# Sequence transform first on untransposed input, and DMA transposes for most of the MLP's input, in a gated FFT/MLP kernel

## The chip, the cores and the metric

The kernel runs on one core of a Trainium2 chip. The metric is the device time of one execution in microseconds (us). The profile's span is the time from the first to the last instruction of the core.

Engine names are those of the profile: PE is the matrix engine, PEld its weight loads, ACT, DVE and POOL are the scalar, vector and GpSimd engines, SP is the engine that does nothing but issue DMA in these kernels (its timeline shows nothing else). A "q" behind a name (SPq) stands for DMA issues on that engine's queue. R, PX and `w_sb` are shared buffers, so one name can stand for several tensors.

## The reference

```python
# x [2048, 512], w_r and w_i [2048, 257], w1 [512, 1792], w2 [1792, 512], all bf16
g = sigmoid((x * gate_w).sum(-1, keepdims=True))
X = rfft2(x.astype(float32)) * (w_r + 1j * w_i)
a = irfft2(X, s=(2048, 512)).astype(bfloat16)
h = x @ w1 + b1
b = (h * tanh(softplus(h))) @ w2          # Mish between two matmuls
return g * a + (1 - g) * b
```

## The kernel before

The two-dimensional FFT is done by matmuls with constant matrices. The d-transform goes over the 512 features. The sequence of 2048 is split as 128 × 16: the p-transform goes over 128 positions, and a "middle stage" does the 16 that remain and multiplies with W. The data between p-transform and middle stage has to change its layout, and goes through a DRAM scratch buffer for that. After the middle stage it goes through a second scratch buffer, and the inverse transforms follow. PE is filled with MLP matmuls wherever the transform chain waits.

A list scheduler in Python plans the order of instructions on each engine when the kernel is built. It knows only modelled durations, and sees the DMA as one first-in first-out pipe with a fixed rate. The planned order is then built into the program.

```python
DMA_BW = 390e3                       # planner's idea of the DMA rate, bytes per us
...
x_sb = R1[:].rearrange("p (t d) -> p t d", t=NT)          # 16 tiles of x, 128 rows each
...
# w1 and x: loads on SP's queue
t_w1 = ld_w1(1)                      # the last of them
# constants (W_r, W_i, SM; then w2, GD), GpSimd's queue, start when t_w1 has landed
wload("wr", Wa, A_w_r, "Wa")
wload("wi", Wb, A_w_i, "Wb")
dma("ld_sm", SM[:], ..., deps=[t_w1], queue="pool")
for h in range(2):
    dma(f"ld_w2_{h}", ..., deps=[t_w1], queue="pool")
dma("ld_gd", GD[:], ..., deps=[t_w1], queue="pool")
```

Each tile is first transposed on PE. Its sums and differences (butterflies) and its d-transform work on the transposed tile, then the p-transform follows:

```python
for t in range(NT):
    ...
    for dt_ in range(4):             # PE transposes (L598), then an eviction to xT on DVE or ACT
        ins = e.transpose(psb[:, bk(sl), 128*dt_:128*(dt_+1)], x_sb[:, t, 128*dt_:128*(dt_+1)], ident[:, :])
    ...
    bfly("bd", XB[:, 2:4, tr_, :], xT[:, 0:2, tr_, :], xT[:, 2:4, tr_, :], ALU.subtract, ...)
    bfly("bs", xss, xT[:, 0:2, tr_, :], xT[:, 2:4, tr_, :], ALU.add, ...)
    ...
# d-transform (L633 to L636): writes runs of 64 neighbouring PSUM columns
e.matmul(o[:, :, 2:4, :], XB[:, 2, t, :], f4(256), start=True, stop=False)
e.matmul(o[:, :, 2:4, :], XB[:, 3, t, :], f4(512), start=False, stop=True)
e.matmul(o[:, :, 0, :], XB[:, 0, t, :], f2(0), start=True, stop=True)
return e.matmul(o[:, :, 1, :], XB[:, 1, t, :], f2(128), start=True, stop=True)
# eviction, then the p-transform (L645)
return e.matmul(ps[:, bk(sl), :], FT[:, t, :], In1[:, t, :], start=True, stop=True)
# eviction; every fourth tile a scratch write
dma(f"r1w{t // 4}", scr1_w[...], A1s[...], 128 * 4096, ...)
```

The gate needs the transposed form of the whole of x, and so does the MLP:

```python
for t in range(NT):                  # gate, L664: 64 small matmuls as one task
    for dt_ in range(4):
        ins = e.matmul(ps[:, bk(sl_g), t:t+1], xT[:, dt_, t, :], gw_sb[:, dt_:dt_+1], ...)
...
for h in range(4):                   # scratch reads
    dma(f"r1r{h}", In2[...], scr1_r[...], 128 * 4096, reads=[("scr1", i) for i in range(4)], ...)
# first middle-stage matmul, L733
e.matmul(ps[:, bk(sx), 0:256], MI["RFe"], In2[:, 0, :], start=True, stop=True)
...
# first MLP layer, L785: one "group" is four of these; Mish is L793; second layer is L803
ins = e.matmul(ps[:, bk(sl), :], w1_sb[:, dt_, 128*ft:128*(ft+1)], xT[:, dt_, 4*c:4*c+4, :], ...)
```

## Time and profile before

| | before |
|---|---|
| time, median of 3 runs | 153.02 us (152.56 to 154.95) |
| span of the profiled run | 151.8 us |
| PE busy | 92% of the span |
| share of the chain of waits on PE | 86% |
| first middle-stage matmul | 51.0 us |

From the page of the kernel before: the span, three rows of its slice table (40 slices of 3.8 us, a digit is tenths), the chain by engine, two groups (line, engine, operation, count, then busy us and mean ns, then idle time before them), and one kind of DMA issue (count, size, median us to landing).

```profile
span 151.8 us, 2262 instructions
...
PE   0479998979999999999999999999999999999990
...
PEclk9999998799999999999999999999999999999999
DMA  4999399999993920303030399013010000101011
...
PE 86%; ACT 6%; DMA 4%; DVE 2%; issue 0%; SPq 0%; DVEq 0%
...
L785 PE MATMUL ps<-xT,w_sb 128*128 128x512 bf16 x224 | 52.8, 383 | 1.1 <-ACT hsb L793 1.0
...
L598 PE MATMUL ps<-ident,R 128*128 128x128 bf16 x64 | 5.8, 247 | 6.1 <-DMA R<-in_A_x_dram 6.0
...
scr<-R SPq DMA_DIRECT2D x8, 512.0 KB, 6.7
```

PE is near full from the tenth slice to the end. A PE that is full and on the chain for 86% of the span is the bound. What a change of the front part can win lies in the first nine slices alone. The 6.1 us ahead of the transposes (L598) are waits for x. The DMA is near full in eleven of the first fourteen slices, up to about 53 us.

Two further views show what the front part ends with. First the chain of waits of the kernel before, in order of time (start us, length us, what, count):

```profile
40.65 10.38 PE ps L785 x48
51.03 0.26 PE ps L733
...
124.18 24.19 PE ps L803 x112
```

Then one line of its waits (who, for what, total us, times, longest us):

```profile
PEld ps L733 <- DMA R<-scr: 0.5, 1, 0.5
```

PE does MLP groups until 51.03 us and then starts the middle stage, whose weight load (PEld) waits 0.5 us for the scratch read.

### The profile page before, as it was taken

To read this page: it belongs to the slowest core of one execution; us is meant where nothing else is said; L and a number is where in the kernel's file an instruction comes from. 1 tells how busy PE (TensorE), PEld (TensorE's weight loads), DVE (VectorE), ACT (ScalarE), POOL (GpSimd) and SP (SyncE) were. 2 spreads that over 40 slices of the span, in tenths; PEclk is the share of its full clock that TensorE was granted. 3 is DMA by queue.
4 is the path that set the end of the run, shared out by engine and by line. 5 is a ranking of instruction groups with operands and counts; after the bars stand their busy time and mean duration, and the time that the engine had idled before them with its cause. 6 is when DMAs were issued, how large, how long until landed. Compare 5 with 4: busy or idle time off the path is not lost.

```text
span 151.8 us, 2262 instructions
## 1 busy us (share of the span) xinstructions
PE 139.3 (92%) x850; PEld 73.0 (48%) x850; DVE 79.6 (52%) x173; ACT 75.5 (50%) x125; POOL 11.1 (7%) x21
## 2 busy tenths in 40 slices
PE   0479998979999999999999999999999999999990
PEld 0345666633444444444444445666676444444440
DVE  0183699769400487995954003899679301123111
ACT  2043884699787573433475863254798770000000
POOL 1050694001000000000000000000000000000000
PEclk9999998799999999999999999999999999999999
DMA  4999399999993920303030399013010000101011
GB/s 124 320 420 358 71 248 212 148 220 395 397 293 76 384 104 0 138 0 138 0 138 4 147 278 266 0 69 118 24 71 4 0 0 0 69 0 69 22 52 71
DMA packets 14207, 20.68 MB, mean 136 GB/s; under 512 B 788, under 2 KB 10420, under 8 KB 14132
## 3 DMA queue, kind: packets, MB, share of 16 engines
q1 hardware_dynamic: 12544, 14.81, 29.2%
q0 software_dynamic: 1328, 5.38, 13.5%
q10 hardware_dynamic: 324, 0.33, 1.0%
q8 instruction: 7, 0.11, 0.3%
q14 instruction: 4, 0.03, 0.1%
HBM read 14.23 MB, written 6.29 MB: 135 GB/s over the span
## 4 chain that ended last, share of the span: by engine, by line
PE 86%; ACT 6%; DMA 4%; DVE 2%; issue 0%; SPq 0%; DVEq 0%
PE ps L803 32%; PE ps L785 31%; PE ps L851 5%; DMA R<-in_A_x_dram 4%; ACT R L509 3%; PE ps L832 2%; PE ps L598 2%; PE ps L759 2%; PE ps L735 2%; PE ps L760 2%; PE ps L633 2%; PE ps L634 1%; ACT hsb L793 1%; PE ps L664 1%; PE ps L645 1%; ACT L793 1%
## 5 line engine op out<-in xcount | busy, mean ns | idle before, releaser
L785 PE MATMUL ps<-xT,w_sb 128*128 128x512 bf16 x224 | 52.8, 383 | 1.1 <-ACT hsb L793 1.0
L803 PE MATMUL ps<-w_sb,hsb 128*128 128x512 bf16 x224 | 51.0, 379 | 0.0
L793 ACT ACTIVATE hsb<-ps,b1f 128x512 bf16<-128x512 f32 x56 | 37.9, 689 | 11.5 <-PE ps L785 11.1
L803 PEld LDWEIGHTS ps<-w_sb,hsb 128*128 128x128 bf16 x224 | 21.7, 98 | 24.9
L785 PEld LDWEIGHTS ps<-xT,w_sb 128*128 128x128 bf16 x224 | 21.3, 99 | 25.4 <-ACT hsb L793 2.3
L509 ACT ACTIVATE R<-ps 128x512 bf16<-128x512 f32 (+1 forms) x27 | 15.6, 595 | 13.6 <-PE ps L760 7.1
L508 DVE CAST R<-ps 128x512 bf16<-128x512 f32 (+1 forms) x21 | 14.0, 689 | 11.6 <-PE ps L760 6.4
L882 DVE SCALAR_TENSOR_TENSOR R<-ps,omg,R 128x512 bf16<-128x512 f32 x8 | 6.0, 750 | 23.6 <-PE ps L803 23.6
L746 DVE TENSOR_TENSOR PX<-ps,Wa 128x256 bf16<-128x256 f32 x32 | 11.9, 414 | 10.8 <-PE ps L734 10.5
L746 DVE TENSOR_TENSOR PX<-ps,Wb 128x256 bf16<-128x256 f32 x32 | 11.9, 412 | 0.0
L598 PE MATMUL ps<-ident,R 128*128 128x128 bf16 x64 | 5.8, 247 | 6.1 <-DMA R<-in_A_x_dram 6.0
L813 ACT ACTIVATE R<-ps,omg 128x512 bf16<-128x512 f32 x8 | 5.5, 687 | 10.3 <-PE ps L803 10.3
L842 ACT ACTIVATE TT<-ps 128x512 bf16<-128x512 f32 x13 | 7.5, 593 | 4.9 <-PE ps L832 3.2
L851 PE MATMUL ps<-GD,TT 128*128 128x256 bf16 x64 | 8.9, 273 | 0.0
L598 PEld LDWEIGHTS ps<-ident,R 128*128 128x128 bf16 x64 | 4.7, 112 | 7.3 <-DMA R<-in_A_x_dram 6.3
L874 DVE SCALAR_TENSOR_TENSOR R<-ps,gcol,PX 128x256 bf16<-128x256 f32 x16 | 7.7, 482 | 0.6
L607 ACT ACTIVATE xT<-ps 128x512 bf16<-128x512 bf16 x11 | 5.8, 612 | 4.2 <-PE ps L598 4.1
L875 DVE SCALAR_TENSOR_TENSOR R<-ps,ngcol,PX 128x256 bf16<-128x256 f32 x16 | 7.6, 475 | 0.0
L851 PEld LDWEIGHTS ps<-GD,TT 128*128 128x128 bf16 x64 | 6.1, 98 | 2.8 <-ACT TT L842 0.2
L839 DVE CAST TT<-ps 128x512 bf16<-128x512 f32 x3 | 2.0, 685 | 9.5 <-PE ps L832 9.5
L859 DVE SCALAR_TENSOR_TENSOR PX<-ps,gcol,R 128x512 f32<-128x512 f32 x8 | 6.0, 744 | 1.3 <-PE ps L851 1.3
L633 PE MATMUL ps<-FD,R 128*128 128x256 bf16 x16 | 5.4, 341 | 1.1 <-DVE R L618 1.1
(95 smaller groups left out, 105.4 us busy)
## 6 DMA issues: line engine op xcount, KB each, us to landing
scr<-R SPq DMA_DIRECT2D x8, 512.0 KB, 6.7
R<-scr SPq DMA_DIRECT2D x8, 512.0 KB, 5.5
out_dram<-R SPq DMA_DIRECT2D x8, 256.0 KB, 2.0
w_sb<-in_B_w_dram SPq DMA_DIRECT2D x2, 896.0 KB, 9.4
w_sb<-in_B_w_dram POOLq DMA_DIRECT2D x2, 896.0 KB, 17.9
R<-in_A_x_dram SPq DMA_DIRECT2D x3, 512.0 KB, 9.1
SM<-c_sm POOLq DMA_DIRECT2D x1, 640.0 KB, 14.4
Wa<-in_A_w_r_dram POOLq DMA_DIRECT2D x1, 514.0 KB, 5.5
```

The lines of the kernel that those rows point to most:

```text
L508: G.add(name, [("dve", dve_dur(n), lambda e: e.tensor_copy(out=outf(), in_=inf())), ("act", act_dur(n), lambda e: e.activation(outf(), inf ...
L509: ("act", act_dur(n), lambda e: e.activation(outf(), inf(), AF.Copy))],
L598: ins = e.transpose(psb[:, bk(sl), 128 * dt_:128 * (dt_ + 1)], x_sb[:, t, 128 * dt_:128 * (dt_ + 1)], ident[:, :])
L633: e.matmul(o[:, :, 2:4, :], XB[:, 2, t, :], f4(256), start=True, stop=False)
L746: ins = e.tensor_tensor(out=po, in0=px, in1=pw, op=ALU.mult)
L785: ins = e.matmul(ps[:, bk(sl), :], w1_sb[:, dt_, 128 * ft:128 * (ft + 1)], xT[:, dt_, 4 * c:4 * c + 4, :], start=(dt_ == 0), stop=(dt_ == 3))
L793: return e.activation(hsb[:, hb, ft, :], ps[:, bk(sl), :], AF.Mish, bias=b1f[:, ft:ft + 1])
L803: ins = e.matmul(ps[:, bk(sl), :], hsb[:, hb, ft, 128 * tl:128 * (tl + 1)], w2_sb[:, ft, :], start=(ft == 0), stop=(ft == NFT - 1))
L842: return e.activation(TT[:, st.i, :, :].rearrange("p a b -> p (a b)"), ps[:, bk(sk), :], AF.Copy)
L851: ins = e.matmul(ps[:, bk(sy), 256 * hh:256 * (hh + 1)], TT[:, st.i, i, :], GD[:, i, :], start=(i % 2 == 0), stop=(i % 2 == 1))
L874: e.scalar_tensor_tensor(out=ya[:, t, 0:256], in0=ps[:, bk(sy), 256:512], scalar=gcol[:, t:t + 1], in1=tE[:, se.i, 0:256], op0=ALU.mult, o ...
L875: return e.scalar_tensor_tensor(out=ya[:, t, 256:512], in0=ps[:, bk(sy), 256:512], scalar=ngcol[:, t:t + 1], in1=hi, op0=ALU.mult, op1=ALU ...
```

## The change

Its intent is to start the transform chain earlier. If the p-transform goes first, it contracts over the rows of x and needs no transposed input. The four 128-column matmuls per tile use the butterflied tile as the stationary operand, so their output comes out transposed, as the d-transform wants it. Then only the gate and the MLP need xT, and 12 of its 16 tiles are fetched by transposing DMA instead of PE transposes with evictions. The d-transform can write its outputs in natural column order with strides of 2 and 4, and the multiplies with W become simple 512-column operations. Two smaller things change with it: the first loads are reordered, and Mish no longer waits for the gate's tanh.

The diff, cut to its core:

```diff
+XBAR_BW = 230e3
...
         t_w1 = ld_w1(1)
+        for t in range(4, NT):
+            dma(f"ld_xt{t}", xT[:, :, t, :], xv[:, t, :], 128 * 1024, writes=[("xT", t)], bw=XBAR_BW, transpose=True)
...
-        for t in range(NT):
+        def tr(t):                     # PE transpose of one tile and its eviction, as before
...
+            if t < 4:
+                tr(t)
...
-                bfly("bs", xss, xT[:, 0:2, tr_, :], xT[:, 2:4, tr_, :], ALU.add, 256 * n, xr, [("xs", hv)])
+                xa, xb = x_sb[:, tr_, 0:256], x_sb[:, tr_, 256:512]
+                t_x1.append(bfly("bs", xss, xa, xb, ALU.add, 256 * n, xr, [("xs", hv)]))
...
+            def f_s1(e, t=t, sl=sl):   # p-transform first, output transposed
+                for i in range(4):
+                    ins = e.matmul(ps[:, bk(sl), 128 * i:128 * (i + 1)], XB[:, t, i, :], FT[:, t, :], start=True, stop=True)
...
             def f_a1(e, t=t, sl=sl):
-                e.matmul(o[:, :, 2:4, :], XB[:, 2, t, :], f4(256), start=True, stop=False)
-                e.matmul(o[:, :, 2:4, :], XB[:, 3, t, :], f4(512), start=False, stop=True)
-                e.matmul(o[:, :, 0, :], XB[:, 0, t, :], f2(0), start=True, stop=True)
-                return e.matmul(o[:, :, 1, :], XB[:, 1, t, :], f2(128), start=True, stop=True)
+                e.matmul(o[:, :, 1::2], In1[:, t, 256:384], fd(256, 256), start=True, stop=False)
+                e.matmul(o[:, :, 1::2], In1[:, t, 384:512], fd(512, 256), start=False, stop=True)
+                e.matmul(o[:, :, 0::4], In1[:, t, 0:128], fd(0, 128), start=True, stop=True)
+                return e.matmul(o[:, :, 2::4], In1[:, t, 128:256], fd(128, 128), start=True, stop=True)
...
-                G.add(f"{nm}_{gp}", [("dve", 2 * dve_dur(256), f_w)], ...)
+                G.add(f"{nm}_{gp}", [("dve", dve_dur(512), f_w)], ...)
...
-                G.add(f"hs_{c}_{ft}", ..., reads=[sl, "b1f", "gth"], ...)
+                G.add(f"hs_{c}_{ft}", ..., reads=[sl, "b1f"], ...)
...
-                    ins = e.matmul(..., T2r[:, 2 * t + pl, 128 * hh:128 * (hh + 1)], GT[:, t, :], ...)
+                    ins = e.matmul(..., T2r[:, 2 * t + pl, hh::2], GT[:, t, :], ...)
```

The transposing DMAs stand on SP's queue behind the loads of x and w1 and ahead of the scratch writes. The planner plans them at 230 GB/s in an otherwise orderly pipe. So it puts the gate, which needs all of them, after only 5 of the MLP's groups.

More of the change, by code (lines that the diff above doesn't have):

```diff
@@ L21 @@
 BIDX = {t: i for i, t in enumerate(BGRP)}
-KOFF = (0, 2, 1, 3)
 def _bf16_bits(a):
@@ L198, in _build_consts @@
     c2, s2 = trig(n, 4 * q + 2)
-    ko = np.concatenate([4 * q + 1, 4 * q + 3], axis=1)
+    ko = 2 * np.arange(128)[None, :] + 1
     blocks = [c0, s0, c2, s2]
@@ L223, in _build_consts @@
     GD = np.zeros((128, 4, 256))
-    ke = np.concatenate([4 * np.arange(64), 4 * np.arange(64) + 2])[:, None]
-    ko = np.concatenate([4 * np.arange(64) + 1, 4 * np.arange(64) + 3])[:, None]
+    ke = 2 * np.arange(128)[:, None]
+    ko = ke + 1
     for h, kk in enumerate((ke, ko)):
@@ L436, in _build @@
         ident = sb("ident", [128, 128], BF)
-        xs = PX[:, 0:2048].rearrange("p (h j k) -> p h j k", h=2, j=2)
+        xs = PX[:, 0:2048].rearrange("p (h t k) -> p h t k", h=2, t=4)
         P1 = PX[:, 0:1536].rearrange("p (i k) -> p i k", i=3)
@@ L443, in _build @@
         In2 = R1[:].rearrange("p (j k) -> p j k", j=32)
-        XB = R2[:].rearrange("p (j t s) -> p j t s", j=4, t=NT)
+        XB = R2[:].rearrange("p (t j s) -> p t j s", j=4, t=NT)
         T2 = R2[:].rearrange("p (j k) -> p j k", j=32)
@@ L481, in bk, with dma @@
             return s.i if s.pool is fpool else 4 + s.i
-        def dma(name, dst, src, nbytes, reads=(), writes=(), deps=(), is_out=False, prio=None, queue="sp", bw=DMA_BW):
-            t = G.add(name, [(queue, {"sp": 0.46, "act": 0.46, "pool": 1.0}[queue], lambda e: e.dma_start(dst, src))],
+        def dma(name, dst, src, nbytes, reads=(), writes=(), deps=(), is_out=False, prio=None, queue="sp", bw=DMA_BW, transpose=False):
+            start = (lambda e: e.dma_start_transpose(dst, src)) if transpose else (lambda e: e.dma_start(dst, src))
+            t = G.add(name, [(queue, {"sp": 0.46, "act": 0.46, "pool": 1.0}[queue], start)],
                       reads=reads, writes=writes, deps=deps, prio=PR["ld"] if prio is None else prio)
@@ L525, in ld_w1 @@
             return dma(f"ld_w1_{h}", w1_sb[:, :, 896 * h:896 * (h + 1)], w1v[:, :, 896 * h:896 * (h + 1)], 128 * 4 * 1792, writes=[("w1", h)])
-        ld_x(0, 1)
+        ld_x(0, 2)
+        dma("ld_ft0", FT[:, 0:4, :], d_c["FT"][:, 0:4, :], 128 * 1024, writes=[("FT", 0)], queue="act")
+        ld_x(2, 4)
         dma("ld_fd", FD[:], d_c["FD"][:], 128 * 1536, writes=["FD"], queue="act")
-        ld_x(1, 4)
-        dma("ld_ft0", FT[:, 0:4, :], d_c["FT"][:, 0:4, :], 128 * 1024, writes=[("FT", 0)], queue="act")
+        ld_x(4, 8)
+        dma("ld_ft1", FT[:, 4:16, :], d_c["FT"][:, 4:16, :], 128 * 3072, writes=[("FT", 1), ("FT", 2), ("FT", 3)], queue="act")
         ld_w1(0)
@@ L533, in _build @@
         dma("ld_gw", bgraw[14:18, :], gate_w.rearrange("(dt p) -> dt p", p=128), 1024, writes=["gwraw"], queue="act")
-        ld_x(4, 8)
-        dma("ld_ft1", FT[:, 4:16, :], d_c["FT"][:, 4:16, :], 128 * 3072, writes=[("FT", 1), ("FT", 2), ("FT", 3)])
         ld_x(8, 12)
@@ L588, in _build @@
         wl = []
-        t_tr, t_a1, t_s1, t_r1w, t_s1e = [], [], [], [], []
-        for t in range(NT):
+        def tr(t):
             sl = fslot()
@@ L599, in f_tr @@
                 return ins
-            t_tr.append(G.add(f"tr{t}", [("pe", pe_dur(128, 4), f_tr)], reads=[("x", t), "ident"], writes=[sl], slots=[sl], prio=PR["tr"]))
+            t_x1.append(G.add(f"tr{t}", [("pe", pe_dur(128, 4), f_tr)], reads=[("x", t), "ident"], writes=[sl], slots=[sl], prio=PR["tr"]))
             def f_evx(e, t=t, sl=sl):
@@ L609, in _build @@
             G.add(f"evx{t}", [("dve", 0.43, f_evx), ("act", 0.6, f_evx_a)], reads=[sl], writes=[("xT", t)], prio=PR["tr"] + 0.2)
+        t_x1, t_a1, t_s1, t_r1w = [], [], [], []
+        for t in range(NT):
+            if t < 4:
+                tr(t)
             if t in BGRP:
@@ L613, in _build @@
                 hv = BIDX[t] % 2
-                xss = xs[:, hv, :, 0:128 * n].rearrange("p j (t s) -> p j t s", t=n)
+                xss = xs[:, hv, 0:n, :]
                 tr_ = slice(t0, t0 + n)
@@ L618, in bfly @@
                     ff = lambda e: e.tensor_tensor(out=o, in0=a, in1=b, op=op)
-                    G.add(f"{nm}{t}", [("dve", dve_dur(cols, 2), ff), ("pool", pool_dur(cols), ff)], reads=reads, writes=writes, prio=PR["a1"])
-                xr = [("xT", i) for i in range(t0, t0 + n)]
-                bfly("bd", XB[:, 2:4, tr_, :], xT[:, 0:2, tr_, :], xT[:, 2:4, tr_, :], ALU.subtract, 256 * n, xr, [("XB", 1, t)])
-                bfly("bs", xss, xT[:, 0:2, tr_, :], xT[:, 2:4, tr_, :], ALU.add, 256 * n, xr, [("xs", hv)])
@@ L624, in _build @@
-                bfly("br0", XB[:, 0, tr_, :], xss[:, 0], xss[:, 1], ALU.add, 128 * n, [("xs", hv)], [("XB", 0, t)])
-                bfly("br2", XB[:, 1, tr_, :], xss[:, 0], xss[:, 1], ALU.subtract, 128 * n, [("xs", hv)], [("XB", 2, t)])
+                    return G.add(f"{nm}{t}", [("dve", dve_dur(cols, 2), ff), ("pool", pool_dur(cols), ff)], reads=reads, writes=writes, prio=PR["a1"])
+                xr = [("x", i) for i in range(t0, t0 + n)]
+                xa, xb = x_sb[:, tr_, 0:256], x_sb[:, tr_, 256:512]
@@ new lines, in _build @@
+                t_x1.append(bfly("bs", xss, xa, xb, ALU.add, 256 * n, xr, [("xs", hv)]))
+                bfly("br0", XB[:, tr_, 0, :], xss[:, :, 0:128], xss[:, :, 128:256], ALU.add, 128 * n, [("xs", hv)], [("XB", 0, t)])
+                bfly("br2", XB[:, tr_, 1, :], xss[:, :, 0:128], xss[:, :, 128:256], ALU.subtract, 128 * n, [("xs", hv)], [("XB", 2, t)])
+                t_x1.append(bfly("bd", XB[:, tr_, 2:4, :].rearrange("p t a b -> p t (a b)"), xa, xb, ALU.subtract, 256 * n, xr, [("XB", 1, t)]))
@@ L626, in _build @@
         for t in range(NT):
             sl = fslot()
-            def f_a1(e, t=t, sl=sl):
-                o = ps[:, bk(sl), :].rearrange("p (c m q) -> p c m q", c=2, m=4)
-                f2 = lambda a: FD[:, a:a + 128].rearrange("p (c q) -> p c q", c=2)
-                f4 = lambda a: FD[:, a:a + 256].rearrange("p (c m q) -> p c m q", c=2, m=2)
-                e.matmul(o[:, :, 2:4, :], XB[:, 2, t, :], f4(256), start=True, stop=False)
-                e.matmul(o[:, :, 2:4, :], XB[:, 3, t, :], f4(512), start=False, stop=True)
-                e.matmul(o[:, :, 0, :], XB[:, 0, t, :], f2(0), start=True, stop=True)
-                return e.matmul(o[:, :, 1, :], XB[:, 1, t, :], f2(128), start=True, stop=True)
@@ L638, in _build @@
-            to = min(i for i in BGRP if i >= t)
-            t_a1.append(G.add(f"a1_{t}", [("pe", pe_dur(256, 2) + pe_dur(128, 2), f_a1)],
-                              reads=[("XB", i, to) for i in range(3)] + ["FD"], writes=[sl], slots=[sl], prio=PR["a1"]))
-            evac(f"e1_{t}", lambda t=t: In1[:, t, :], lambda sl=sl: ps[:, bk(sl), :], 512, [sl], [("In1", t)], PR["a1"] + 0.2)
-            sl = fslot()
-            def f_s1(e, t=t, sl=sl):
-                return e.matmul(ps[:, bk(sl), :], FT[:, t, :], In1[:, t, :], start=True, stop=True)
@@ L647, in _build @@
-            t_s1.append(G.add(f"s1_{t}", [("pe", pe_dur(512), f_s1)], reads=[("In1", t), ("FT", t // 4)], writes=[sl], slots=[sl], prio=PR["s1"]))
-            evac(f"e2_{t}", lambda t=t: A1s[:, t, :], lambda sl=sl: ps[:, bk(sl), :], 512, [sl], [("A1s", t)], PR["s1"] + 0.2)
+            def f_s1(e, t=t, sl=sl):
+                ins = None
+                for i in range(4):
+                    ins = e.matmul(ps[:, bk(sl), 128 * i:128 * (i + 1)], XB[:, t, i, :], FT[:, t, :], start=True, stop=True)
+                return ins
@@ new lines, in _build @@
+            to = min(i for i in BGRP if i >= t)
+            t_s1.append(G.add(f"s1_{t}", [("pe", pe_dur(128, 4), f_s1)], reads=[("XB", i, to) for i in range(3)] + [("FT", t // 4)],
+                              writes=[sl], slots=[sl], prio=PR["s1"]))
+            evac(f"e1_{t}", lambda t=t: In1[:, t, :], lambda sl=sl: ps[:, bk(sl), :], 512, [sl], [("In1", t)], PR["s1"] + 0.2)
+            sl = fslot()
+            def f_a1(e, t=t, sl=sl):
+                o = ps[:, bk(sl), :].rearrange("p (c k) -> p c k", c=2)
+                fd = lambda a, n: FD[:, a:a + n].rearrange("p (c q) -> p c q", c=2)
+                e.matmul(o[:, :, 1::2], In1[:, t, 256:384], fd(256, 256), start=True, stop=False)
+                e.matmul(o[:, :, 1::2], In1[:, t, 384:512], fd(512, 256), start=False, stop=True)
+                e.matmul(o[:, :, 0::4], In1[:, t, 0:128], fd(0, 128), start=True, stop=True)
+                return e.matmul(o[:, :, 2::4], In1[:, t, 128:256], fd(128, 128), start=True, stop=True)
@@ L649, in _build @@
+            t_a1.append(G.add(f"a1_{t}", [("pe", pe_dur(256, 2) + pe_dur(128, 2), f_a1)], reads=[("In1", t), "FD"],
+                              writes=[sl], slots=[sl], prio=PR["a1"]))
+            evac(f"e2_{t}", lambda t=t: A1s[:, t, :], lambda sl=sl: ps[:, bk(sl), :], 512, [sl], [("A1s", t)], PR["a1"] + 0.2)
             if t % 4 == 3:
@@ L677, in _build @@
             dma(f"r1r{h}", In2[:, 8 * h:8 * h + 8, :].rearrange("p j k -> p (j k)"), scr1_r[:, 2048 * h:2048 * (h + 1)], 128 * 4096,
-                reads=[("scr1", i) for i in range(4)], writes=[("In2", h)], deps=t_tr, prio=PR["ld"] + 1)
+                reads=[("scr1", i) for i in range(4)], writes=[("In2", h)], deps=t_x1, prio=PR["ld"] + 1)
         sl_t = fslot()
@@ L721, in _build @@
         G.add("uze", [("dve", 0.2, lambda e: e.tensor_copy(out=T2[:, :, 0], in_=ps[:, bk(sl_u), 0:32]))],
-              reads=[sl_u], writes=["T2z"], deps=t_a1, prio=PR["mid"] + 0.5)
-        wvv = {id(W): W[:, :, 0:256].rearrange("p j (q a b) -> p j b a q", a=2, b=2) for W in (Wa, Wb)}
+              reads=[sl_u], writes=["T2z"], deps=t_s1, prio=PR["mid"] + 0.5)
         p1pool, p2pool = _Pool(3), _Pool(3)
@@ L740, in f_w @@
                 def f_w(e, W=W, P=P, s_=s_, j0=j0, sx=sx):
-                    ins = None
-                    for jj in range(2):
-                        px = ps[:, bk(sx), 256 * jj:256 * (jj + 1)].rearrange("p (b a q) -> p b a q", b=2, a=2)
-                        pw = W[:, j0 + jj, 0:256].rearrange("p (q a b) -> p b a q", a=2, b=2)
-                        po = P[:, s_.i, 256 * jj:256 * (jj + 1)].rearrange("p (b a q) -> p b a q", b=2, a=2)
-                        ins = e.tensor_tensor(out=po, in0=px, in1=pw, op=ALU.mult)
-                    return ins
-                G.add(f"{nm}_{gp}", [("dve", 2 * dve_dur(256), f_w)], reads=[sx] + rd, writes=[s_], slots=[s_], prio=PR["mid"] + 0.2)
+                    return e.tensor_tensor(out=P[:, s_.i, :].rearrange("p (j k) -> p j k", j=2), in0=ps[:, bk(sx), :].rearrange("p (j k) -> p j k", j=2),
+                                           in1=W[:, j0:j0 + 2, 0:256], op=ALU.mult)
+                G.add(f"{nm}_{gp}", [("dve", dve_dur(512), f_w)], reads=[sx] + rd, writes=[s_], slots=[s_], prio=PR["mid"] + 0.2)
             su = fslot()
@@ L765, in _build @@
                         [su], [("T2", gp)], PR["mid"] + 0.4)
-            G.tasks[-1].deps.extend(x for x in t_a1 if x not in G.tasks[-1].deps)
+            G.tasks[-1].deps.extend(x for x in t_s1 if x not in G.tasks[-1].deps)
             if gp % 4 == 3:
@@ L772, in _build @@
             dma(f"r2r{h}", T2r[:, 8 * h:8 * h + 8, :], scr2_r[:, 8 * h:8 * h + 8, :], 128 * 4096,
-                reads=[("scr2", i) for i in range(4)], writes=[("T2r", h)], deps=t_s1, prio=PR["ld"] + 1)
+                reads=[("scr2", i) for i in range(4)], writes=[("T2r", h)], deps=t_a1, prio=PR["ld"] + 1)
         late = []
@@ L793, in f_hs @@
                     return e.activation(hsb[:, hb, ft, :], ps[:, bk(sl), :], AF.Mish, bias=b1f[:, ft:ft + 1])
-                G.add(f"hs_{c}_{ft}", [("act", act_dur(512, True), f_hs)], reads=[sl, "b1f", "gth"], writes=[("hs", hb, ft)], prio=PR["act"] - c)
+                G.add(f"hs_{c}_{ft}", [("act", act_dur(512, True), f_hs)], reads=[sl, "b1f"], writes=[("hs", hb, ft)], prio=PR["act"] - c)
             for tl in range(4):
@@ L831, in f_s1i @@
                     pl, hh = i % 2, i // 2
-                    ins = e.matmul(ps[:, bk(sk), 128 * i:128 * (i + 1)], T2r[:, 2 * t + pl, 128 * hh:128 * (hh + 1)], GT[:, t, :], start=True, stop=True)
+                    ins = e.matmul(ps[:, bk(sk), 128 * i:128 * (i + 1)], T2r[:, 2 * t + pl, hh::2], GT[:, t, :], start=True, stop=True)
                 return ins
```

## The prediction

> **What bounds the kernel now.** TensorE, once it is fed. In the slice table PE is at 90% or more from 34 us to 148 us, and the chain of waits is 86% PE (MLP matmuls alone 63%). Their steady rate in the chain is 0.216 us per 512-column matmul. The loss is in the first 35 us: 4.6 us until x arrives, a second wait to 6.6 us, half clock (matmuls at 0.21 us for 256 columns instead of 0.11), and around 22-24 us and 28.5-35 us waits for PSUM evictions, mostly on ACT (0.60 us each), and for its 1.28 us table load. The transform chain then needs its scratch round trip: the first middle matmul starts at 51.0 us, right when the scratch read lands. DMA is about full from 17 to 54 us.
>
> **What the change does.** It removes 48 of 64 PE transposes (0.057 us each back to back: 2.7 us of PE) and 12 xT evictions (0.42 us DVE or 0.61 us ACT), and starts the first transform directly after the butterflies on x. So I expect the transform stage to end near 22-25 us instead of 35. The p-transform becomes four 128-column matmuls (about 0.22 us, as before). The d-transform now writes PSUM with strides 2 and 4; [...] this trace has none to check, I allow 0 to 5 us, mostly hidden. The merged 512-column multiplies save nothing much (0.67 us cadence per pair now). Two extra ACT table loads (1.28 us each) appear, because Tanh comes between Mish activations.
>
> It adds 12 DMA transposes (1.5 MB), queued behind the x and w1 loads, which land near 16 us, and ahead of the scratch writes. The instruction order shows the gate matmuls after only 5 of the 28 first MLP groups, and they wait for all 12. PE gets there near 23 us. Alone, the transposes should take about 7 us: 256-byte packets take 18 ns on one of 16 engines in this trace. But the constants' loads start near 17.9 us, [...] from 34 to 41 us the 512-byte scratch writes got only 0.15 of the engines beside 4096-byte packets. With equal 4 KB turns I estimate landing near 30 us; with 256-byte turns beyond 40.
>
> **Sum.** After the gate PE has 25 us of work (gate 1.8, 23 groups of 0.86, 14 second-layer matmuls) before the first middle matmul; about 94.3 us remain from there (100.8 now, less 6.5 us of MLP work moved ahead); 1.2 us separate span and time. Landing at 30 us, with 1.5 us for table loads and cold clock, gives about 152. Floor: the scratch round trip, pushed by 1.5 MB more traffic, reaches the first middle matmul at about 52-55 us, so 148 to 151. So the front gain is mostly given back as a PE wait at the gate.
>
> Predicted 152.5 us, range 148 to 162; faster by over 2% 0.24, within 2% 0.48, slower 0.28.
>
> **Right or wrong in the profile.** Transform stage done by about 25 us; a PE wait of 4-10 us before the 64 gate matmuls, released by a transposing DMA; the first middle matmul at 54-58 us instead of 51.0; PE full from there; from it to the end about 95 us; tail unchanged (about 24 us of second-layer matmuls).
>
> **What would make it wrong.** Transposes landing before 26 us (faster, about 148), or starved until the constants are in at 41 us (up to 165); strided PSUM writes stretching the first stage past the gate; half clock after the stall; middle stage, with less filler, becoming DVE-bound.

The sum is 30 + 1.5 + 25 + 94.3 + 1.2 = 152 us. But the two landing times are estimates for two assumed sizes of a turn; of the sharing between queues only the 0.15 was measured then. The 0 to 5 us for the strides are the allowance, with no measurement behind it. The two table loads did come: 1.28 us each in the kernel after, at 32.85 us ahead of the gate's tanh and at 55.09 us ahead of Mish.

## The result, and the profile after

The changed kernel takes 175.32 us in the median of 4 runs (174.32 to 178.81); the kernel before takes 153.06 us (152.56 to 154.95) in the same rounds. The ratio is 1.1445, with a 95% interval of 1.1369 to 1.1521. Ratios here and below are the mean time of one kernel's fast runs over that of the other's fast runs of the same rounds, so they are not quite the ratio of the medians quoted. Executions over 1.5% slower than the fastest of the same kernel are left out of the means.

From the page of the kernel after, the lines that answer to those of the page before:

```profile
span 173.9 us, 2233 instructions
...
PE   0696998100008999999999999999999999999992
...
PEclk9999999955555799999999999999999999999999
DMA  4999995999999493000030211398113000011011
...
PE 68%; SPq 26%; DMA 3%; issue 1%; DVE 0%
...
L675 PE MATMUL ps<-gw_sb,xT 128*128 128x1 bf16 x64 | 1.8, 165 | 21.5 <-DMA xT<-in_A_x_dram 21.5
```

The hole is in plain sight. PE does nothing in slices 9 to 12 (a slice is 4.35 us here), and the gate (L675) is what ends it: PE stood idle for 21.5 us before it, for a transposing DMA. The span grew by 22.1 us, so the hole is about all of it. The granted clock was 0.50 from 34.7 to 58.6 us, in and after the hole; this costs nothing while PE waits, and some 2 us when it starts again (27.2 us, in the windows below, for work that the prediction counts as 25 us).

What PE did around the hole is told by the windows of the kernel after (from:to us, length, then busy us and count of PE, PEld, DVE, ACT and POOL, then granted clock, DMA share and GB/s):

```profile
31.00:52.60 21.60, 0.12 (x1) 0.00 (x0) 0.00 (x0) 3.11 (x5) 0.00 (x0) 0.59 1.08 212
52.60:79.80 27.20, 27.14 (x180) 13.09 (x181) 5.04 (x6) 17.59 (x27) 0.00 (x0) 0.89 0.45 146
```

In the first stretch the DMA engines are fully taken, and the compute engines have run dry, but for the last evictions and activations on ACT. In the second PE is full: 27.14 us of 27.20.

The chain of waits of the kernel after, in order of time:

```profile
20.87 7.85 SPq L484
...
28.77 14.61 SPq L484
...
43.42 4.13 SPq L484
...
47.59 4.93 DMA xT<-in_A_x_dram
52.66 1.85 PE ps L675 x64
54.50 18.52 PE ps L790 x76
...
76.81 3.02 PE ps L808 x14
...
146.34 24.19 PE ps L808 x112
```

Before 47.59 us the chain is SP's issues ("SPq"), three of which take long. The last transpose is issued at 47.59 us and lands at 52.5. After the gate, PE goes through MLP groups and second-layer matmuls. Its first middle-stage matmul (L743) starts at 79.83 us, 28.8 us later than before. From there to the end of the span it is 94.1 us, where it was 100.8: the 6.7 us are MLP work that now lies ahead of it (126 matmuls instead of 96, at 0.216 us each 6.5 us). The sum of the two, 28.8 - 6.7 = 22.1 us, is the growth of the span.

What SP's queue did is in the timeline of SP in the kernel after (start us, length us, what, count):

```profile
4.54 44.32 SPq L484 DMA_TRANSPOSE xT<-in_A_x_dram  x12
49.04 5.05 SPq L484 DMA_DIRECT2D scr<-R  x4
59.66 1.76 SPq L484 DMA_DIRECT2D R<-scr  x4
```

SP was in these twelve issues until 48.9 us. It could only then issue the four scratch writes, whose data was there by about 30 us (the transform stage ended at 29.4). So the scratch trip was held up too. But it was hidden: the scratch reads ended at 67.5 us, before PE had gone through its planned filler (79.8 us).

The lengths of single issues are in the view of the tile xT of the kernel after (count, then min/median/max ns, then first and last start in us):

```profile
L484 SPq DMA_TRANSPOSE xT<-in_A_x_dram x12: 1268/1578/14609, 4.5 to 47.6; - x12
```

The shortest of these twelve issues took 1.27 us, the longest 14.6 us.

### The profile page after: what moved, and what is told of

It is laid out like the page before. It is cut to its first block, busy times and chain, and to the rows that moved or that the text cites. A ratio compares the mean times of both kernels' runs of the same rounds, so it can differ in the third digit from the quotient of the medians.

```text
span 173.9 us, 2233 instructions
## 1 busy us (share of the span) xinstructions
PE 140.7 (81%) x850; PEld 74.7 (43%) x850; DVE 75.7 (44%) x131; ACT 75.0 (43%) x121; POOL 18.3 (11%) x25
## 4 chain that ended last, share of the span: by engine, by line
PE 68%; SPq 26%; DMA 3%; issue 1%; DVE 0%
PE ps L808 28%; PE ps L790 27%; SPq L484 26%; PE ps L856 4%; DMA xT<-in_A_x_dram 3%; PE ps L837 2%; PE ps L764 2%; PE ps L745 2%; PE ps L765 2%; PE ps L675 1%; DVE R L887 0%; PE ps L698 0%; PE ps L699 0%; PE ps L763 0%; PE ps L760 0%
## 5 line engine op out<-in xcount | busy, mean ns | idle before, releaser
L790 PE MATMUL ps<-xT,w_sb 128*128 128x512 bf16 x224 | 54.4, 390 | 0.7 <-ACT hsb L798 0.7
L790 PEld LDWEIGHTS ps<-xT,w_sb 128*128 128x128 bf16 x224 | 21.8, 100 | 25.7 <-issue 2.8
L675 PE MATMUL ps<-gw_sb,xT 128*128 128x1 bf16 x64 | 1.8, 165 | 21.5 <-DMA xT<-in_A_x_dram 21.5
L751 DVE TENSOR_TENSOR PX<-ps,Wa 128x512 bf16<-128x512 f32 x16 | 10.9, 684 | 7.2 <-PE ps L744 6.5
L675 PEld LDWEIGHTS ps<-gw_sb,xT 128*128 128x128 bf16 x64 | 1.8, 104 | 22.0 <-issue 22.0
L751 DVE TENSOR_TENSOR PX<-ps,Wb 128x512 bf16<-128x512 f32 x16 | 10.9, 681 | 0.0
L847 ACT ACTIVATE TT<-ps 128x512 bf16<-128x512 f32 x14 | 8.1, 593 | 3.4 <-PE ps L856 1.7
L640 PE MATMUL ps<-FT,R 128*128 128x128 bf16 x64 | 5.6, 242 | 2.7 <-DVE R L625 2.6
L653 PE MATMUL ps<-FD,R 128*128 128x256 bf16 x16 | 7.0, 439 | 0.0
## 6 DMA issues: line engine op xcount, KB each, us to landing
SM<-c_sm POOLq DMA_DIRECT2D x1, 640.0 KB, 22.6
```

The source lines that it names most:

```text
L653: e.matmul(o[:, :, 1::2], In1[:, t, 384:512], fd(512, 256), start=False, stop=True)
L751: return e.tensor_tensor(out=P[:, s_.i, :].rearrange("p (j k) -> p j k", j=2), in0=ps[:, bk(sx), :].rearrange("p (j k) -> p j k", j=2), in ...
L790: ins = e.matmul(ps[:, bk(sl), :], w1_sb[:, dt_, 128 * ft:128 * (ft + 1)], xT[:, dt_, 4 * c:4 * c + 4, :], start=(dt_ == 0), stop=(dt_ == 3))
L847: return e.activation(TT[:, st.i, :, :].rearrange("p a b -> p (a b)"), ps[:, bk(sk), :], AF.Copy)
```

## The experiments

The kernel before was run with each set on the same chip; its medians were 152.93 to 153.33 us. The theory at the start was this: **the transposes are starved by the constants' loads, because they go in 256-byte pieces and the queues take turns piece by piece** (an assumption then; the counts below test it). The rivals: the transposes are slow by themselves; or SP's issues, and not the traffic, hold them; or the slow first stage (strided PSUM writes) causes the loss.

### Plain copies in the place of transposes, in pieces of 256 and 1024 bytes

The first edit takes the transposition away but keeps bytes, destination, queue and 256-byte pieces. The second also changes the layout of xT, so that the pieces have 1024 bytes. The result of both kernels is wrong (xT isn't transposed; relative error 0.07).

```diff
 # plain256
-            dma(f"ld_xt{t}", xT[:, :, t, :], xv[:, t, :], ..., transpose=True)
+            dma(f"ld_xt{t}", xT[:, :, t, :], xv[:, t, :].rearrange("p (a b) -> p a b", a=4), ...)
 # plain1024
-        xT = sb("xT", [128, 4, NT, 128], BF)
+        xTr = sb("xT", [128, NT, 4, 128], BF)
+        xT = xTr[:].rearrange("p t a b -> p a t b")
-            dma(f"ld_xt{t}", xT[:, :, t, :], xv[:, t, :], ..., transpose=True)
+            dma(f"ld_xt{t}", xTr[:, t, :, :].rearrange("p a b -> p (a b)"), xv[:, t, :], ...)
```

> The changed kernel with its 12 transposing DMAs replaced by plain copies of the same bytes in the same 256-byte pieces, on the same queue at the same place; every engine's instruction order is unchanged and the result is wrong on purpose. Theory P (turns by packet: a 256-byte packet gets one turn for each packet of the constants' queue, whatever its size): the copies land nearly as late as the transposes did (52.5 us), the gate still waits 15 us or more, time 168 to 176 us. Rival X (the transposing itself is slow, or upsets the other queue): the copies land before 32 us, no long gate wait, time 152 to 157 us.

> The same with plain copies in 1024-byte pieces (a quarter of the packets; the transposed x is laid out tile by tile so that a piece is contiguous; wrong result on purpose). Theory P: only 96 packets per engine instead of 384, about half of them through before the constants start, so they land near 24 us, the gate wait of 21.5 us goes to under 2 us, time about 153 us (150 to 156). Rival X expects the same as for the 256-byte copies, since neither transposes; if both are fast it is X, if only this one is fast it is P.

Measured: plain256 takes 168.92 us (167.63 to 170.41), ratio 1.0987 [1.0884, 1.109]. plain1024 takes 152.77 us (152.55 to 154.08), ratio 0.999 [0.9894, 1.0086]. The group of the gate in plain256, from its groups by form:

```profile
L675 PE MATMUL ps<-gw_sb,xT 128*128 128x1 bf16 x64 | 1.8, 165 | 14.3 <-DMA xT<-in_A_x_dram 14.3
```

In plain256 the wait is still 14.3 us: the last piece arrived at 45.3 us, without any transposition. In plain1024 the copies were done at 19.5 us, and the gate (31.1 us) did not wait at all. The group of the gate in plain1024 shows it:

```profile
L676 PE MATMUL ps<-gw_sb,xT 128*128 128x1 bf16 x64 | 1.7, 164 | 0.0
```

So it isn't transposition as such: most of the loss comes with plain copies too if their pieces are small (the wait is a little under the 15 us that I had expected as the least). It is also not the order of the plan, which is the same in all three kernels.

How the turns are taken can be counted from the trace's records of DMA packets. Each row is one microsecond from the span's start, all 16 engines together, by the pieces that start in it; in the first four rows both queues are busy:

```
kernel, us          software queue (constants)        SP's queue
after, 44-45        80 of 4096 bytes, 0.94 of time    81 of  256 bytes, 0.11 of time
plain256, 39-40     80 of 4096 bytes                  86 of  256 bytes
late_xpose, 53-54   80 of 4096 bytes                  81 of  256 bytes (a run further below)
before, 36-37       84 of 4096 bytes, 0.87 of time    95 of  512 bytes, 0.16 of time (scratch writes)
queue alone:
after, 15-16                                         928 of  256 bytes, 238 GB/s
plain1024, 17-18                                     342 of 1024 bytes
```

In the first four rows it is one piece for one piece, though their sizes differ by a factor of 8 or 16. Counts alone would also fit turns of several pieces each, but the start times don't: in the kernel before, from 35 to 41 us, 494 of 508 large pieces have a small one starting 3 to 4 ns before their end (by chance, with the times shifted by some ns, 61 to 84 have). In the kernel after it is 869 small pieces beside 798 of the constants from 26 to 47 us. It is not so everywhere: from 20 to 26 us, beside the first constants, it is 735 beside 145, and no run shows why.

Beside 4096-byte pieces, the queue of 256-byte pieces moved 81 × 256 bytes per us = 21 GB/s in the kernel after, under a tenth of the 238 GB/s that it moved alone. The counts and the start times fit a turn of one record, be it of 256, 512 or 4096 bytes.

A limit of plain1024 has to be told. Its copies were over (19.5 us) before the first piece of the constants moved (20.2 us). So it shows that this load, with its larger pieces, slipped through the gap ahead of the constants, and not what 1024-byte pieces would get beside them.

### The constants behind the transposes

The same kernel, with the same order on every engine, but GpSimd's loads wait for the last transpose. The outputs are right.

```diff
         order = G.schedule()
+        byname = {t.name: t for t in G.tasks}
+        byname["ld_wrp"].deps.append(byname["ld_xt15"])
```

> The changed kernel with one wait more: the constants' loads on the GpSimd queue start only when the last transposing DMA has landed; instruction order unchanged on every engine. Theory P: alone the transposes take about 7 us, so they land near 23 us, the gate starts when PE gets there (about 31 us) and waits for nothing; first middle matmul near 58 us, 94 us from there, time 152 to 157 us. Rival S (the issuing queue is the limit: 1.3 us and more for each transposing DMA, whoever else loads): landing stays after 30 us and the gate still waits.

Measured: 156.49 us (156.45 to 157.35), ratio 1.0218 [1.0145, 1.0291]. From its view of the tile xT:

```profile
L484 SPq DMA_TRANSPOSE xT<-in_A_x_dram x12: 1267/1268/4662, 4.6 to 25.3; - x12
```

Without the constants' traffic the twelve transposes go from 14.5 to 27.6 us, the gate starts at 31.1 us, and PE doesn't wait before it. That is the starvation theory's main test, and it held, though the landing was expected near 23 us. It also shows an error of the prediction: "alone, the transposes should take about 7 us" was wrong. They took 13 us, and the median issue is 1268 ns: twelve of them are 15 us of SP's time, while the DMA engines were busy for only 0.68 of that stretch. So the issues were the limit, not the engines. 1.57 MB in 13.1 us are 120 GB/s. The rate was higher for moments (1023 pieces, 262 GB/s, from 16 to 17 us), and lower later (88 GB/s in the page's slice from 19.5 to 23.3 us, all queues together). The issue of a plain copy of the same bytes took less: 0.54 us in the median in plain1024, and 1.06 us in plain256, which had the constants' loads beside it.

It also shows where the next wall stands. From the chain of const_after:

```profile
30.77 24.98 DMA scr<-R
55.83 3.94 DMA R<-scr
59.82 0.28 PE ps L743
```

Now the scratch writes in 512-byte pieces stand beside the constants' loads, which run later than before. They take until 55.8 us, and the middle stage can't start before 59.8 (PE, which has filler until shortly before, waits 1.2 us for it). What one transfer was spared, the next one pays.

### All transposes on PE, as before

This keeps the new order of transforms and the strides, but makes all of xT on PE. The outputs are right.

```diff
-        for t in range(4, NT):
+        for t in range(NT, NT):           # no transposing DMA
             dma(f"ld_xt{t}", ...)
...
-            if t < 4:
+            if t < NT:
                 tr(t)
```

> The changed kernel with all 16 tiles of x transposed on TensorE as before, none by DMA; the scheduler may reorder. All that is left of the change is the p-transform first on natural x and the natural column order. If the DMA transposes are the whole loss: no long gate wait, 149 to 155 us, that is within 2% of the kernel before. If the new order or the strided PSUM writes cost as such (0.65 us per tile for the d-transform instead of 0.33 us, 5 us in all): 155 to 160 us.

Measured: 154.65 us (154.2 to 155.03), ratio 1.0083 [1.0013, 1.0153]. The gate starts at 36.3 us and the first middle matmul at 51.7, where it was 51.0 before. So the DMA transposes are worth about 20 us of loss, and the rest of the change about one more.

### The old column order, with unstrided PSUM writes

Two kernels take back the column order (block order of k, the constants FD and GD, the multiplies with W and the inverse weights): one with the DMA transposes, one with all on PE.

```diff
-                e.matmul(o[:, :, 1::2], In1[:, t, 256:384], fd(256, 256), start=True, stop=False)
-                e.matmul(o[:, :, 1::2], In1[:, t, 384:512], fd(512, 256), start=False, stop=True)
-                e.matmul(o[:, :, 0::4], In1[:, t, 0:128], fd(0, 128), start=True, stop=True)
-                return e.matmul(o[:, :, 2::4], In1[:, t, 128:256], fd(128, 128), start=True, stop=True)
+                e.matmul(o[:, :, 2:4, :], In1[:, t, 256:384], f4(256), start=True, stop=False)
+                e.matmul(o[:, :, 2:4, :], In1[:, t, 384:512], f4(512), start=False, stop=True)
+                e.matmul(o[:, :, 0, :], In1[:, t, 0:128], f2(0), start=True, stop=True)
+                return e.matmul(o[:, :, 1, :], In1[:, t, 128:256], f2(128), start=True, stop=True)
```

> The changed kernel with the old block order of the k columns, so that the d-transform writes PSUM in contiguous runs of 64 and more columns; the DMA transposes stay. If the strided writes halve the d-transform's rate (0.216 us for 256 columns at full clock against 0.108 before), the transform stage ends 4 to 5 us earlier, but the gate still waits for the last transpose near 52 us, so the time stays within 2% of the changed kernel, 172 to 178 us. If the strided writes are a part of the 22 us, it falls below 170 us.

> All 16 tiles transposed on TensorE and the old block order of the k columns: of the change only the p-transform first on natural x is left. Against the run with all on TensorE and strided writes (154.65 us), 16 tiles times 0.33 us less d-transform: about 149.5 us (148 to 152) if the strided writes cost their 5 us once nothing hides them; 154 to 155 us if the scratch round trip (first middle matmul at 51.7 us there, behind a DMA) hides them.

First, do the strides cost anything? The timeline of PE in the kernel before, for one tile's d-transform at full clock (granted 1.00; start us, length us, line):

```profile
20.46 0.27 PE L633 MATMUL ps<-FD,R 128*128 128x256 bf16 x1
20.57 0.27 PE L634 MATMUL ps<-FD,R 128*128 128x256 bf16 x1
20.68 0.22 PE L635 MATMUL ps<-FD,R 128*128 128x128 bf16 x1
...
20.79 0.27 PE L633 MATMUL ps<-FD,R 128*128 128x256 bf16 x1
```

And the same in the kernel after, also at a granted clock of 1.00:

```profile
24.81 0.42 PE L653 MATMUL ps<-FD,R 128*128 128x256 bf16 x1
25.02 0.31 PE L654 MATMUL ps<-FD,R 128*128 128x128 bf16 x1
25.14 0.31 PE L655 MATMUL ps<-FD,R 128*128 128x128 bf16 x1
25.24 0.42 PE L652 MATMUL ps<-FD,R 128*128 128x256 bf16 x1
```

Matmuls overlap, so the rate is read from start to start: 0.11 us for 256 columns before (20.46 to 20.57), 0.21 us after (24.81 to 25.02). The strided write ran at half the rate here. A whole tile takes 0.33 us before (20.46 to 20.79) and 0.65 us after (27.84 to 28.49 in the same timeline); over 16 tiles I estimate from this 5 us of PE. So it was a factor of two, for 4-byte elements at stride 2.

Then, does it matter? contig took 175.53 us in its one fast run (the other three, 178.85 to 179.57, were slow, so no ratio is given); the kernel after took 175.32. From the groups by form of contig:

```profile
L653 PE MATMUL ps<-FD,R 128*128 128x256 bf16 x16 | 5.6, 347 | 0.0
...
L676 PE MATMUL ps<-gw_sb,xT 128*128 128x1 bf16 x64 | 1.8, 165 | 22.2 <-DMA xT<-in_A_x_dram 22.2
```

The matmuls of L653 got faster (347 ns in the mean, 439 in the kernel after), and the wait for the transposes grew from 21.5 to 22.2 us. The strides are real but hidden behind the gate's wait.

pe_all_contig was the miss among these. I hoped that it would show the gain of the reordering at last. It took 156.65 us (155.4 to 157.71), ratio 1.0239 [1.016, 1.0318]. That is outside both of the ranges that I had given, and rather slower than pe_all. One line of its waits:

```profile
PE ps L744 <- DMA R<-scr: 4.9, 1, 4.9
```

And its chain:

```profile
29.23 18.24 DMA scr<-R
47.56 4.11 DMA R<-scr
51.71 0.39 PE ps L744
```

In pe_all PE waited 1.2 us at this place, here 4.9 us, and the first middle matmul starts at 51.7 us in both. The time that the unstrided writes saved was waited away here, and after this wait the granted clock was half from 51.3 to 54.7 us (0.66 in the mean from 50 to 55 us), which it was not in pe_all (1.00). The transform stage is quicker now, and the scratch writes aren't: their last byte lands at 47.1 us beside the constants' loads, as in the kernel before (46.6). **The scratch trip, not the transform stage, sets the start of the middle stage.** That is why the whole intent of the change, an earlier transform stage, cannot pay by itself.

### Loads that nobody needs yet, behind the scratch writes

If that is so, making the scratch writes land earlier must start the middle stage earlier. w2, GD and GT aren't needed until then, and can wait. The base is pe_all_contig.

```diff
+        for t_ in G.tasks:
+            if t_.name in ("ld_w2_0", "ld_w2_1", "ld_gd"):
+                t_.deps.extend(t_r1w)              # t_r1w: the four scratch writes
-        dma("ld_gt", ..., deps=t_s1, queue="pool")
+        dma("ld_gt", ..., deps=t_s1 + t_r1w, queue="pool")
```

> As the last, and the loads of w2, GD and GT on the GpSimd queue wait until the four scratch writes have landed. By theory P the 512-byte scratch writes are starved by the 4096-byte packets of w2 just as the transposes were; without them they land near 34-37 us instead of 46-47, the first middle matmul comes at 42-46 us, and the wait of TensorE in front of it goes: 148 to 150 us. If the scratch writes are not starved by these loads: no earlier than 50 us.

Measured: 151.62 us median; the fast runs 150.98 to 152.12, one slow run 155.88; ratio 0.9894 [0.9842, 0.9947]. The last byte of the scratch writes landed at 39.1 us instead of 47.1, and the first middle matmul started at 43.5 us. The mechanism was as expected, but the time missed its range of 148 to 150 us. Another run was to put the DMA transposes where they don't collide: tiles 8 to 15 are DMA-transposed behind the scratch writes, with the gate in two halves.

```diff
+        for t in range(8, NT):
+            dma(f"ld_xt{t}", xT[:, :, t, :], xv[:, t, :], ..., transpose=True, deps=t_r1w)
+        gate_half(0)                     # tiles 0 to 7
+        gate_half(1)                     # tiles 8 to 15
```

> As the last, and x tiles 8 to 15 transposed by DMA, issued behind the scratch reads when no other load is in flight, tiles 0 to 7 on TensorE, the gate in two halves. By theory P a transposing DMA with the queues to itself lands at its issue rate, about 1.3 us each, so all 8 are in by about 56 us, before their tiles are needed; TensorE loses 32 transposes (1.8 us) and 8 evictions, gains two table loads on ACT: 145 to 149 us. If transposing is slow even alone, TensorE waits for it before the second gate half and the time is over 150 us.

Measured: 153.54 us (152.69 to 154.38), ratio 1.0034 [0.997, 1.0097]. That missed too. The place wasn't free either: w2 and the other late loads run there until 56.8 us, the eight issues took 18.3 us (42.8 to 61.1), and the pieces took turns one for one as before (80 beside 81 in a row of the table above). But PE never waited for these tiles. In both kernels PE waited again before the middle stage: 2.7 us in the first, 2.4 us in the second. The middle stage starts some eight and seven us earlier (43.5 and 45.1 us) than in pe_all_contig, but the planner thinks that the scratch trip is quicker still, and gives PE too little MLP work to do until then. In late_xpose the granted clock was half after the wait as well (45.2 to 48.6 us; 0.66 in the mean from 45 to 50 us).

### Filler that fits the trip

So the planner was told a lower rate for the scratch writes (200 GB/s instead of 390), nothing else. It then puts 24 MLP groups, not 18, ahead of the first middle matmul. Three kernels got this: the one with all transposes on PE, the one with late DMA transposes, and, as a control, the kernel before, which got the new load order and the new rate and no part of the change.

```diff
-                                 ..., writes=[("scr1", t // 4)], prio=PR["ld"] + 1))
+                                 ..., writes=[("scr1", t // 4)], prio=PR["ld"] + 1, bw=200e3))
```

> The run with scratch first (all transposes on TensorE, block column order, w2/GD/GT behind the scratch writes), and the planner is told a slower rate for the scratch writes, so that it puts 24 instead of 18 first-layer groups before the first middle matmul. TensorE waited 2.7 us there at 43.5 us; six more groups (5.2 us) fill it, nothing else changes: 148 to 149.5 us, which would beat both kernels by 2.5 to 3%. If that wait was not what kept it from its floor, it stays at 151 to 152 us.

> The kernel with tiles 8 to 15 transposed by DMA behind the scratch reads and the gate in halves, with the same planned rate for the scratch writes. If late DMA transposes pay once TensorE is filled (1.8 us less of TensorE work, 8 evictions fewer): below the filled kernel with all on TensorE, 146 to 148.5 us. If the planner has too little first-layer work left to fill the front, because tiles 8 to 15 are not there: 149 to 153 us.

> The kernel before with the same order of loads (w2, GD and GT behind the scratch writes) and the same planned rate, nothing else changed. It tells whether the gain of the last kernel is the load order alone. The kernel before has TensorE full from 35 us and hardly waits for the scratch read, so an earlier read buys nothing: 151.5 to 154 us. If the load order is the whole gain: 148 to 150 us.

| kernel | median us of all runs (range of the fast runs) | ratio to before | first middle matmul |
|---|---|---|---|
| filled | 151.19 (149.49 to 151.55) | 0.9842 [0.9782, 0.9902] | 45.6 us |
| late_filled | 151.02 (150.36 to 151.74) | 0.9857 [0.9807, 0.9907] | 46.8 us |
| before_scratch_first | 151.10 (150.36 to 151.55, one slow run 152.93) | 0.9858 [0.9797, 0.9919] | 45.7 us |

In all three PE goes into the middle stage without a wait. (In filled it waits 1.3 us later, at 53.4 us, for w2, which the new order delays.) filled was expected at 148 to 149.5 us and missed that; late_filled lies in the range given for too little first-layer work (149 to 153 us), and shows no gain from the late DMA transposes. The control decides: the kernel before, with the two small edits, is as fast as the best kernel with the p-transform first (the intervals overlap), and a little faster than I had expected. So a gain of about 1.5% comes with the load order and the filler and without any part of the change, and p-transform-first adds nothing that these runs could resolve. All three beat the kernel before, but only by about 1.5%.

### Which of the two edits it is

The last run gives the kernel before the new load order alone.

> The kernel before with only the load order changed (w2, GD and GT wait for the scratch writes), the planner's scratch rate left as it was, so that fewer MLP groups (about 17) stand ahead of the first middle matmul. If the load order alone gives the 1.4% of before_scratch_first: 150.5 to 151.7 us. If the gain needs the longer filler as well: PE waits about 2 to 3 us for the scratch read near 42 us, part of it at half clock afterwards, and the time is 151.8 to 153.5 us.

Measured: 152.95 us (152.58 to 153.53), ratio 0.997 [0.9923, 1.0016]. From its timeline of PE, with the idle time before a matmul in brackets:

```profile
38.20 4.48 PE L788 MATMUL ps<-xT,w_sb 128*128 128x512 bf16 x20
44.72 0.28 PE L736 MATMUL ps<-R,SM 128*128 128x256 bf16 x1 [2.04 <-DMA R<-scr]
```

The middle stage starts earlier (44.7 us against 51.0), and the time is the same. PE has the same work to do in both kernels; the earlier middle stage saved nothing by itself, and PE stands idle for 2.04 us because the plan gave it 20 matmuls here, where the same timeline of before_scratch_first has 36:

```profile
37.95 7.93 PE L788 MATMUL ps<-xT,w_sb 128*128 128x512 bf16 x36
```

With these 16 more (four groups of 0.86 us) the wait is gone and about 1.1% of the time (0.997 to 0.986). So the load order alone isn't enough. The filler alone was not run.

One thing is left open by this. The kernel before has no such wait that could be removed: after 35 us its PE is never idle. In the two profiled executions PE's work from the end of the transform stage to its last matmul takes the same 113 us (34.98 to 148.4 us in the kernel before, 32.42 to 145.7 in before_scratch_first). The difference lies ahead of that, where PE goes through the same steps at another rate. In the kernel before it is half until 14.9 us (0.21 us for 256 columns) and again from 25.1 to 28.5 us, where the granted clock is 0.50; in before_scratch_first it is half until 12.3 us only (until 13.0 in before_order_only). From 25 to 35 us the granted clock is 0.83 in the mean in the kernel before, and 1.00 in the other two. One trace of each can't tell whether the edits bring the better clock. So the 1.4% is measured, but where it comes from is not shown.

## Why the prediction was wrong

The prediction was 152.5 us, with a range of 148 to 162, and 0.28 on slower by over 2%. The kernel took 175.3.

**The bound: right.** PE was the bound, and the loss is PE's idle time: 21.5 us in one place.

**The place of the wait: right.** It named the gate, behind five groups of the first layer, waiting for a transposing DMA.

**The step that failed: "With equal 4 KB turns I estimate landing near 30 us; with 256-byte turns beyond 40."** The case was decided for the first half, and the second half is what happened. The trace before already had the evidence, and the prediction quoted it: scratch writes of 512 bytes got 0.15 of the engines beside 4096-byte packets. Equal turns in bytes would have given them about half. Counting records of one microsecond would have shown 95 of 512 bytes beside 84 of 4096. The last transpose landed at 52.5 us, so the wait at the gate was 21.5 us and not the 4 to 10 us that the prediction named.

With that one number put right, the sum holds:

| term | predicted | measured |
|---|---|---|
| transposes landed, gate starts | 30 us | 52.66 us |
| gate to first middle matmul | 25 + 1.5 us | 27.2 us |
| first middle matmul to end of span | 94.3 us | 94.1 us |
| span to time | 1.2 us | 1.4 us |
| sum | 152 us | 175.3 us |

("Span to time" is the median less the profiled span: 175.3 less 173.9. The profiled run itself took 175.59 us.)

**"Alone, the transposes should take about 7 us": wrong.** It was 13 us in const_after, limited by the issues at 1.27 us each. It counted packets and left out that a DMA has to be issued. This alone would have cost nothing: in const_after the gate at 31.1 us didn't wait.

**"Starved until the constants are in at 41 us (up to 165)": right in kind, too small.** The constants' loads were slowed as well; the matrix SM took 22.6 us from issue to landing, where it was 14.4 before, and the constants were in at about 50 us instead of 43. Starvation ended only when the competing loads ended, and beside the transposes these ended later.

**"Transform stage ends near 22 to 25 us": wrong, and without effect.** It ended at 29.4 us. The d-transform at half rate costs about 5 us of PE (the estimate above), and butterflies on DVE were slower while POOL did butterflies at the same time: two of 256 columns took 1.12 and 1.23 us beside POOL's, and two more 0.29 and 0.28 us once POOL was done. The prediction had allowed 0 to 5 us for the strides, mostly hidden: that was right, and contig and pe_all_contig show that removing them gains no time.

**"Floor of 148 to 151 us from the scratch trip": the right wall, and it turned out to be the real one.** pe_all and pe_all_contig hit it at 51.7 us, the middle stage's start.

**What stays open.** The real transposes landed at 52.5 us, the plain copies in the same pieces at 45.3 us. Of these 7.2 us, 5.6 are that the constants' loads ended later: at 50.3 us (50.8 in contig, which also has the transposes), where they ended at 44.7 us beside the plain copies and at 43.3 in the kernel before. So this part comes with the transposing and not with bytes or piece size; in what way isn't shown. The constants' single pieces took longer from 24 to 40 us (those of SM 582 ns in the mean, 391 in contig, against 323 in plain256 and 298 in the kernel before). Three issues of transposes took 7.85, 14.61 and 4.13 us, 26.6 us in all, where the last issue of the plain copies was over at 25.4 us; no run separates that from the rest.

## What to carry to other kernels

Where two DMA queues meet, count their turns too, not their bytes alone: here a queue with 256-byte pieces got 21 GB/s beside one with 4096-byte pieces and 238 GB/s alone, and the gate's wait of 21.5 us went when the bulk load was put behind it (const_after). Before shortening a stage, ask what its consumer waits for last: here the middle stage waited for the scratch trip, so an earlier transform stage bought nothing. And when PE is the bound, an earlier start of a stage need not pay (before_order_only starts it 6.3 us earlier and takes the same time): the filler planned ahead of a transfer has to fit the transfer as measured.
